# q of the first half batch by a hardware queue and cast on ScalarE, q of the last batch by crossbar, key pieces of batch 3 spread, last rows split: a fused Sinkhorn-attention and feed-forward kernel

## Chip, cores, metric

One core of one Trainium2 chip. The metric is device time in microseconds; medians of several executions are given. Ratios are the mean time of one kernel's fast runs over the mean of the other's of the same rounds, so they are not quite the ratio of the medians beside them.

## The reference, cut

```python
# q, k, v: (4, 8, 768, 64); sort_net: (4, 8, 8, 8); 8 blocks of 96 rows
P = sort_net
for _ in range(5):
    P = P - max(P, -1);  P = exp(P)
    P = P / (sum(P, -1) + 1e-9);  P = P / (sum(P, -2) + 1e-9)
k_sorted, v_sorted = P @ blocks of k, P @ blocks of v
attn = softmax(q_b @ k_sorted_b.T / 8) @ v_sorted_b         # within each block
x = heads joined: (3072, 512)
h = relu(x @ w_in)                                          # w_in (512, 2048)
out = (s * h * h + b) @ w_out                               # w_out (2048, 512)
```

## The kernel before, the parts that matter

Tokens come in eight groups of 384 (`t`), two for each batch. `ffn1(t)` and `ffn2(t)` are the two feed-forward layers; attention pieces of later groups are hung between their matmuls by a `Queue`. To evacuate a result is to copy it out of PSUM, where matmuls leave it; a load lands when the profile has its completion count full; its readers start right behind that (q of the changed kernel at 15.84, its first cast at 15.86). Only the opening has no feed-forward work to hide behind.

```python
    sn = sk.tile([BH, NB, NB], FP)
    nc.sync.dma_start(out=sn, in_=sort_net.rearrange("b h i j -> (b h) i j"))
    kb = const.tile([128, BLK, D], BF)
    vb = const.tile([128, 128, D], BF)
    def load_q(b, part=slice(0, 128)):            # q, k, v: GpSimd's (software) queue, cast to bf16 on the way
        if b not in qr:
            qr[b] = qrp.tile([128, H, TQ, D], BF, tag="qr", name=f"qr{b}")
        nc.gpsimd.dma_start(
            out=qr[b][part].rearrange("p h t d -> p h (t d)"),
            in_=q[b].rearrange("h (p t) d -> p h (t d)", t=TQ)[part])
    # ...
    load_q(0, slice(0, 64))
    load_k(*brows(0))
    load_v(*brows(0))
    load_q(0, slice(64, 128))
    # ... masks on GpSimd (ident, emat, bmask, hmask), then the loads of the weights
    between = [lambda: zero_pad(BLK), lambda: zero_pad(BLK + 16), lambda: None,
               lambda: None, lambda: None]
    for it in range(5):                            # Sinkhorn
        nc.scalar.activation(out=sn, in_=sn, func=AF.Exp)
        between[it]()                              # other ScalarE work, in order behind the exp
        # ... seven small VectorE instructions: row sums, column sums, divisions
    # ...
    warm_up(38)                                    # matmuls of zeros, ahead of the real work
    q_half(0, "s")                                 # 48 PE transposes of q, evacuated on ScalarE
    warm_up(12)
    build_pd1()                                    # Sinkhorn result -> operand pd of the key and value matmuls
    k_piece(0, 0, 16, 1, "v")()                    # keys: 16 matmuls, evacuated on VectorE ("v") or ScalarE ("s")
    k_piece(0, 32, 16, 1, "s")()
    # ... two more key pieces, value pieces, scores, q_half(1), ... then ffn1(0)
    # the attention pieces that are hung into ffn2(2) and ffn2(3):
    at4, at5 = attn(4), attn(5)
    for i, n in enumerate((1, 4, 6)):
        at4[n] = K(3, 32 * i, 16, "vsv"[i])
    at5[1] = lambda: q_piece(3, 0, "s")
    at5[4] = lambda: q_piece(3, 2, "v")
    qu = Queue(at4 + at5, 24)
```

The softmax here doesn't subtract the row's maximum and nothing guards it: scores larger than these inputs give would overflow.

Of the kernel before, what the change touches and what calls it, by code (L numbers as in the profile page):

```python
# [9 lines left out]
FP = mybir.dt.float32  # L10
BF = mybir.dt.bfloat16
AF = mybir.ActivationFunctionType
ALU = mybir.AluOpType
# [5 lines left out]
def kernel(  # L19
# [12 lines left out]
    nc = tc.nc  # L32

    B, H, S, D = q.shape
    NB = sort_net.shape[-1]
    BLK = S // NB
    BH = B * H
    NHP = H // 2
    d_model = H * D
    d_ff = moe_w_in.shape[1]  # L40
    NF = d_ff // 128
    HB = NB // 2
    TG = HB * BLK
    NT = B * 2
    VW = D + 2
    TQ = S // 128
# [8 lines left out]
    qrp = ctx.enter_context(tc.tile_pool(name="qrp", bufs=2))  # L55
    qtp = ctx.enter_context(tc.tile_pool(name="qtp", bufs=2))
# [4 lines left out]
    gtp = ctx.enter_context(tc.tile_pool(name="gtp", bufs=2))  # L61
    osb = ctx.enter_context(tc.tile_pool(name="osb", bufs=3))
# [4 lines left out]
    psb = ctx.enter_context(tc.tile_pool(name="psb", bufs=2, space=bass.MemoryType.PSUM))  # L67
# [3 lines left out]
    sn = sk.tile([BH, NB, NB], FP)  # L71
    nc.sync.dma_start(out=sn, in_=sort_net.rearrange("b h i j -> (b h) i j"))

    kb = const.tile([128, BLK, D], BF)
    vb = const.tile([128, 128, D], BF)
    qr = {}

    def load_q(b, part=slice(0, 128)):
        if b not in qr:
            qr[b] = qrp.tile([128, H, TQ, D], BF, tag="qr", name=f"qr{b}")  # L80
        nc.gpsimd.dma_start(
            out=qr[b][part].rearrange("p h t d -> p h (t d)"),
            in_=q[b].rearrange("h (p t) d -> p h (t d)", t=TQ)[part])

    def load_k(rows, prow, n=1):
        for c0 in range(0, BLK, BLK // n):
            cs = slice(c0, c0 + BLK // n)
            nc.gpsimd.dma_start(out=kb[prow, cs, :], in_=kraw[rows, cs, :])
# [4 lines left out]
    def brows(b):  # L93
        return slice(b * 64, (b + 1) * 64), slice((b % 2) * 64, (b % 2) * 64 + 64)

    s_bc = const.tile([128, 1], FP)
# [15 lines left out]
    new_vs(1)  # L112
    nc.scalar.activation(out=warm, in_=warm, func=AF.Exp)

    load_q(0, slice(0, 64))
    load_k(*brows(0))
    load_v(*brows(0))
    load_q(0, slice(64, 128))
# [24 lines left out]
    for c0 in range(0, d_ff, FCH):  # L143
        w = const.tile([128, NHP, FCH], BF, name=f"wi{c0}")
        nc.gpsimd.dma_start(
            out=w, in_=moe_w_in.rearrange("(hp p) f -> p hp f", p=128)[:, :, c0:c0 + FCH])
# [5 lines left out]
    for f0 in range(0, NF, FW):  # L152
        w = const.tile([128, FW, d_model], BF, name=f"wo{f0}")
        nc.gpsimd.dma_start(
            out=w, in_=moe_w_out.rearrange("(f p) n -> p f n", p=128)[:, f0:f0 + FW, :])
# [7 lines left out]
    def wo_at(f):  # L163
        return wos[f // FW][:, f % FW, :]
# [4 lines left out]
    def warm_up(n):  # L169
        for _ in range(n):  # L170
            wp = psb.tile([128, 256], FP, tag="b", name="wp")
            nc.tensor.matmul(out=wp, lhsT=zt[:, 0:128], rhs=zt, start=True, stop=True)  # L172

    def zero_pad(r0):
        nc.scalar.copy(out=vb[:, r0:r0 + 16, :],
                       in_=zt[:, 0:D].unsqueeze(1).broadcast_to([128, 16, D]))
# [4 lines left out]
    nc.vector.tensor_reduce(out=rstat, in_=sn, axis=AX.X, op=ALU.max)  # L181
    nc.vector.tensor_tensor(out=sn, in0=sn, in1=rstat.broadcast_to([BH, NB, NB]),
                            op=ALU.subtract)
    between = [lambda: zero_pad(BLK), lambda: zero_pad(BLK + 16), lambda: None,
               lambda: None, lambda: None]
    for it in range(5):
        nc.scalar.activation(out=sn, in_=sn, func=AF.Exp)
        between[it]()
# [6 lines left out]
        if it == 0:  # L195
            nc.vector.tensor_scalar(out=rstat, in0=rstat, scalar1=1e-9, scalar2=None,
                                    op0=ALU.add)
# [28 lines left out]
    def evac(out, in_, eng):  # L226
        if eng == "v":
            nc.vector.tensor_copy(out=out, in_=in_)  # L228
        else:
            nc.scalar.copy(out=out, in_=in_)  # L230

    QT = {}
# [18 lines left out]
    def q_piece(b, hp0, eng):  # L251

        if hp0 == 0:
            QT[b] = qtp.tile([128, NHP, S], BF, tag="qt", name=f"qt{b}")
        ps = psa.tile([128, 2, 1024], BF, tag="a", name="tq")
        for i in range(2):
            for t in range(TQ):
                for e in range(2):
                    nc.tensor.transpose(  # L259
                        out=ps[e * 64:(e + 1) * 64, i, t * 128:(t + 1) * 128],  # L260
                        in_=qr[b][:, 2 * (hp0 + i) + e, t, :], identity=ident)
        evac(QT[b][:, hp0:hp0 + 2, :].rearrange("q a (p t) -> q a p t", t=TQ),
             ps[:, :, 0:S].rearrange("q a (t p) -> q a p t", t=TQ), eng)

    def k_piece(b, c0, nc2, nb, eng):




        pr = brows(b)[1] if nb == 1 else slice(0, 128)  # L270
        rhs = (pd1[pr] if b < 2 else pd2[pr, b - 2]).rearrange("p e m i -> p (e m i)")
        if nc2 * nb > 8:
            ps = psa.tile([128, nc2, nb * 64], FP, tag="a", name="tk")
        else:
            ps = psb.tile([128, nc2, nb * 64], FP, tag="b", name="tk")
        for c in range(nc2):
            nc.tensor.matmul(out=ps[:, c, :],  # L277
                             lhsT=kb[pr, c0 + 2 * c:c0 + 2 * c + 2, :].rearrange("p c d -> p (c d)"),
                             rhs=rhs, start=True, stop=True)
        g0 = (b % 2) * 32  # L280

        def half(cp):
            if b == 0:
                cs = slice(c0 + cp, c0 + 2 * nc2, 2)
            else:
                cs = slice(cp * (BLK // 2) + c0 // 2, cp * (BLK // 2) + c0 // 2 + nc2)
            for e in range(2):
                evac(ks[e * 64:(e + 1) * 64, g0:g0 + nb * 32, cs].rearrange(
                         "p (b g) c -> p b g c", b=nb),
                     ps[cp * 64:(cp + 1) * 64].rearrange(  # L290
                         "p c (b e g) -> p e b g c", b=nb, e=2)[:, e], eng)

        half(0)
        return lambda: half(1)
# [133 lines left out]
    GT = {}  # L428
# [22 lines left out]
    bias = const.tile([128, d_model], FP)  # L451
# [3 lines left out]
    def flush():  # L455
        while waiting:
            r0, ops = waiting.pop(0)
            ot = osb.tile([128, d_model], FP, tag="ot", name="ot")
            nc.vector.scalar_tensor_tensor(out=ot, in0=ops, scalar=s_bc, in1=bias,  # L459
                                           op0=ALU.mult, op1=ALU.add)  # L460
            nc.sync.dma_start(out=out[r0:r0 + 128, :], in_=ot)

    def ffn2(t, slot=nothing):
        gt = GT.pop(t)
        for m in range(TG // 128):
            ops = psb.tile([128, d_model], FP, tag="b", name="ops")
            for f in range(NF):
                nc.tensor.matmul(out=ops, lhsT=gt[:, f, m * 128:(m + 1) * 128],  # L468
                                 rhs=wo_at(f), start=(f == 0), stop=(f == NF - 1))
                if f % 4 == 3:  # L470
                    if f == NF - 1:
                        waiting.append((t * TG + m * 128, ops))
                        if ready:
                            flush()
                    slot()
# [22 lines left out]
    def S2(t, hp):  # L498
        return lambda: (s_piece(t, hp), s_piece(t, hp + 1))

    def P2(t, hp):
        return lambda: (p_piece(t, hp), p_piece(t, hp + 1))

    def T(t):
        return lambda: x_turn(t)

    def attn(t):
        return [S2(t, 0), nothing, P2(t, 0), S2(t, 2), nothing, P2(t, 2), nothing, T(t)]
# [9 lines left out]
    def build_pd1():  # L518
        pt = block_rows(0)
        nc.vector.tensor_tensor(  # L520
            out=pd1, in0=hmask.rearrange("p (m e) i -> p e m i", e=2),
            in1=bass.AP(tensor=pt.tensor, offset=pt.offset,
                        ap=[list(pt.ap[0]), [0, 2], [0, NHP], list(pt.ap[1])]),
            op=ALU.mult)
# [9 lines left out]
                op=ALU.mult)  # L534


    warm_up(38)
    q_half(0, "s")
    warm_up(12)
    build_pd1()  # L540
    k_piece(0, 0, 16, 1, "v")()
    k_piece(0, 32, 16, 1, "s")()
    k_piece(0, 64, 8, 1, "v")()
# [40 lines left out]
    def csums(f0, f1):  # L584
        for f in range(f0, f1):
            if f == 1:
                nc.gpsimd.tensor_tensor(out=csum, in0=wo_at(0), in1=wo_at(1), op=ALU.add)
            elif f > 1:
# [9 lines left out]
    qu = Queue([lambda: q_piece(1, 0, "s"), lambda: q_piece(1, 2, "v")]  # L598
               + [lambda c0=c0: k_piece(1, c0, 16, 1, "vsv"[c0 // 32])() for c0 in range(0, BLK, 32)]
               + [seq(lambda: load_k(*brows(2)), lambda: load_k(*brows(3)), lambda: load_q(2), bias_piece), S2(2, 0), V2[0], S2(2, 2), V2[1], V2[2], V2[3],  # L600
                  P2(2, 0), V2[4], P2(2, 2), V2[5], S2(3, 0),
                  T(2), P2(3, 0), S2(3, 2), lambda: q_piece(2, 0, "v"), P2(3, 2), T(3),
                  lambda: q_piece(2, 2, "v")], 24)
# [3 lines left out]
    def K(b, c0, nc2, eng):  # L607
        return lambda: k_piece(b, c0, nc2, 1, eng)()

    qu = Queue([nothing if i % 2 else K(2, i * 8, 8, "vs"[i // 2 % 2]) for i in range(12)]  # L610
               + [nothing] * 4, 16)
# [4 lines left out]
    v_read(2, nc.gpsimd)  # L616
    v_read(3, nc.gpsimd)
    load_q(3)
    at4, at5 = attn(4), attn(5)
    for i, n in enumerate((1, 4, 6)):  # L620
        at4[n] = K(3, 32 * i, 16, "vsv"[i])
    at5[1] = lambda: q_piece(3, 0, "s")
    at5[4] = lambda: q_piece(3, 2, "v")
    qu = Queue(at4 + at5, 24)
    ffn2(2, qu)
    ffn2(3, qu)
    ffn1(4)
# [1 line left out]
    qu = Queue(attn(6) + attn(7), 24)  # L629
# [36 lines left out]
```

## Time and profile before

| | before |
|---|---|
| median | 241.99 us |
| span of the profiled execution | 241.1 us |
| PE busy | 227.1 us (94%) |
| key matmuls of batch 0 start | 13.49 |
| first feed-forward matmul | 30.66 |
| PE clock at half speed | 14.40 to 34.88 |

Times inside a kernel are microseconds from the start of the profiled execution. PE is TensorE, DVE VectorE, ACT ScalarE, POOL GpSimd, SP the sync engine. The views that carry the argument are shown in the prediction; two lines more, from the table of windows of the kernel before (window, length, then busy time of PE, PEld, DVE, ACT, POOL, then clock, DMA share, GB/s), show the stall that the second half of the change is for: 1.23 us of PE idle in the first, 0.32 in the second.

```profile
119.00:134.00 15.00, 13.77 (x154) 7.44 (x155) 8.90 (x18) 6.24 (x9) 0.00 (x0) 1.00 0.16 46
134.00:149.00 15.00, 14.68 (x166) 8.02 (x167) 10.06 (x16) 4.45 (x5) 0.00 (x0) 1.00 0.31 80
```

### The profile page before, as it was taken

To read this page: it belongs to the slowest core of one execution; us is meant where nothing else is said; L and a number is where in the kernel's file an instruction comes from. 1 tells how busy PE (TensorE), PEld (TensorE's weight loads), DVE (VectorE), ACT (ScalarE), POOL (GpSimd) and SP (SyncE) were. 2 spreads that over 40 slices of the span, in tenths; PEclk is the share of its full clock that TensorE was granted. 3 is DMA by queue.
4 is the path that set the end of the run, shared out by engine and by line. 5 is a ranking of instruction groups with operands and counts; after the bars stand their busy time and mean duration, and the time that the engine had idled before them with its cause. 6 is when DMAs were issued, how large, how long until landed. Compare 5 with 4: busy or idle time off the path is not lost.

```text
span 241.1 us, 4882 instructions
## 1 busy us (share of the span) xinstructions
PE 227.1 (94%) x2059; PEld 136.1 (56%) x2080; DVE 134.1 (56%) x268; ACT 107.9 (45%) x154; POOL 39.2 (16%) x52
## 2 busy tenths in 40 slices
PE   8869799989999999999998999999999999999993
PEld 4468698845545555555554455666554556654441
DVE  5775547967993558766465748343353544342221
ACT  6356456435438451677626250656522225660000
POOL 7820000099960000460000000000000000000000
PEclk9965569999999999999999999999999999999998
DMA  4999999985999993599902061400014232001212
GB/s 63 187 199 212 216 201 206 219 206 103 141 153 178 273 307 97 123 120 112 146 7 87 3 152 46 109 0 3 1 52 122 67 111 45 0 3 43 82 48 87
DMA packets 29622, 27.33 MB, mean 113 GB/s; under 512 B 16928, under 2 KB 23840, under 8 KB 29088
## 3 DMA queue, kind: packets, MB, share of 16 engines
q0 software_dynamic: 8400, 15.21, 38.0%
q1 hardware_dynamic: 21200, 11.81, 20.6%
q8 instruction: 16, 0.26, 0.5%
q14 instruction: 6, 0.05, 0.1%
HBM read 29.63 MB, written 8.65 MB: 159 GB/s over the span
## 4 chain that ended last, share of the span: by engine, by line
PE 84%; DVE 6%; DMA 6%; issue 2%; POOL 1%; ACT 1%; POOLq 0%
PE hps L442 34%; PE ops L468 34%; DMA vb<-in_v_dram 6%; PE sc L358 3%; PE pv L385 3%; PE tv L303 2%; PE tk L277 2%; PE tq L259 2%; DVE x L390 2%; PE tv L333 1%; DVE gt L447 1%; DVE vn L228 1%; DVE ot L459 1%; PE tq L244 1%; DVE ks L228 1%
## 5 line engine op out<-in xcount | busy, mean ns | idle before, releaser
L442 PE MATMUL hps<-xt,wi 128*128 128x384 bf16 (+1 forms) x576 | 89.8, 313 | 1.0 <-DVE xt L228 1.0
L468 PE MATMUL ops<-wo,gt 128*128 128x512 bf16 x363 | 87.7, 380 | 1.5 <-issue 0.5
L446 ACT ACTIVATE rt<-hps 128x768 bf16<-128x768 f32 (+1 forms) x72 | 53.2, 739 | 53.7 <-PE hps L442 52.6
L442 PEld LDWEIGHTS <-wi 128*128 128x128 bf16 x576 | 54.6, 100 | 31.3 <-issue 2.3
L447 DVE TENSOR_TENSOR gt<-rt 128x768 bf16<-128x768 bf16 (+1 forms) x72 | 42.0, 585 | 42.2 <-ACT rt L446 41.8
L468 PEld LDWEIGHTS <-gt 128*128 128x128 bf16 x384 | 35.0, 98 | 38.4 <-issue 0.6
L361 ACT ACTIVATE at<-sc 96x768 bf16<-96x768 f32 x32 | 24.3, 802 | 35.2 <-PE sc L358 35.2
L459 DVE SCALAR_TENSOR_TENSOR ot<-ops,s_bc,bias 128x512 f32<-128x512 f32 x24 | 18.0, 749 | 38.0 <-PE ops L468 37.9
L390 DVE TENSOR_TENSOR x<-pv,rec 96x512 bf16<-96x512 f32 (+1 forms) x36 | 22.6, 628 | 1.3
L228 DVE CAST ks<-tk 64x512 bf16<-64x512 f32 (+1 forms) x36 | 20.9, 579 | 4.2 <-PE tk L277 3.8
L589 POOL TENSOR_TENSOR csum<-csum,wo 128x512 f32<-128x512 f32 x14 | 17.6, 1254 | 1.0
L230 ACT CAST ks<-tk 64x256 bf16<-64x256 f32 (+1 forms) x28 | 13.7, 490 | 8.0 <-PE tk L277 7.7
L385 PEld LDWEIGHTS <-at 96*128 96x128 bf16 (+1 forms) x256 | 12.3, 105 | 4.0 <-ACT qt L230 1.0
L385 PE MATMUL pv<-vs,at 96*128 96x66 bf16 (+1 forms) x256 | 13.0, 200 | 0.8 <-DVE rec L389 0.6
L358 PEld LDWEIGHTS <-ks 64*96 64x96 bf16 x256 | 8.4, 132 | 6.8 <-issue 5.0
L389 DVE RECIPROCAL rec<-pv 96x8 f32<-96x8 f32 (+1 forms) x36 | 6.9, 192 | 9.2 <-PE pv L385 9.2
L358 PE MATMUL sc<-qt,ks 64*96 64x96 bf16 x256 | 10.8, 223 | 1.0 <-DVE x L390 1.0
L172 PE MATMUL wp<-zt 128*128 128x256 bf16 x50 | 9.1, 300 | 1.1 <-DVE warm L104 1.1
L277 PEld LDWEIGHTS <-kb 64*128 64x128 bf16 x192 | 6.7, 98 | 5.4 <-issue 5.3
L277 PE MATMUL tk<-pd,kb 64*128 64x64 bf16 x192 | 8.2, 195 | 0.9 <-DVE pd L520 0.9
L230 ACT CAST vn<-tv 128x1024 bf16<-128x1024 f32 x6 | 6.1, 1012 | 4.1 <-PE tv L333 2.3
L303 PE MATMUL tv<-pd,vb 64*128 64x64 bf16 x64 | 6.0, 272 | 1.7 <-DMA vb<-in_v_dram 1.1
(67 smaller groups left out, 101.1 us busy)
## 6 DMA issues: line engine op xcount, KB each, us to landing
out_dram<-ot SPq DMA_DIRECT2D x24, 256.0 KB, 2.2
kb<-in_k_dram POOLq DMA_DIRECT2D x4, 768.0 KB, 10.1
vb<-in_v_dram POOLq DMA_DIRECT2D x4, 768.0 KB, 18.9
qr<-in_q_dram POOLq DMA_DIRECT2D x3, 768.0 KB, 19.3
wi<-in_moe_w_in_dram POOLq DMA_DIRECT2D x2, 1024.0 KB, 18.9
wo<-in_moe_w_out_dram POOLq DMA_DIRECT2D x2, 1024.0 KB, 30.1
dv<-vn SPq DMA_DIRECT2D x6, 256.0 KB, 6.6
vs<-dv POOLq DMA_DIRECT2D x4, 384.0 KB, 11.1
```

Of the source, the lines that this page charges most:

```text
L228: nc.vector.tensor_copy(out=out, in_=in_)
L230: nc.scalar.copy(out=out, in_=in_)
L277: nc.tensor.matmul(out=ps[:, c, :], lhsT=kb[pr, c0 + 2 * c:c0 + 2 * c + 2, :].rearrange("p c d -> p (c d)"), rhs=rhs, start=True, stop=True)
L358: nc.tensor.matmul(out=sc[:, e, n * BLK:(n + 1) * BLK], lhsT=ks[pr, g0 + n, :], rhs=QT[b][pr, hp, q0:q0 + BLK], start=True, stop=True)
L361: nc.scalar.activation(out=at, in_=sc[:, :, 0:TG], func=AF.Exp, scale=scale)
L385: nc.tensor.matmul(out=pv[e][0:m, (n - n0) * VW:(n - n0 + 1) * VW], lhsT=atf[:, c0:c0 + m], rhs=VS[b][:, gi, :], start=True, stop=True)
L390: nc.vector.tensor_tensor(out=x[:, n0:n0 + nn, hp * 128:(hp + 1) * 128].rearrange("p n (e d) -> p e n d", e=2), in0=pvv[:, :, :, 0:D], in1 ...
L442: nc.tensor.matmul(out=hps[:, f, 0:nt], lhsT=wi_at(hp, f0 + f), rhs=xt_at(t, hp, n0, nn), start=(hp == 0), stop=(hp == NHP - 1))
L446: nc.scalar.activation(out=rt[:, :, 0:nt], in_=hps[:, :, 0:nt], func=AF.Relu)
L447: nc.vector.tensor_tensor(out=gt[:, f0:f0 + 2, c0:c0 + nt], in0=rt[:, :, 0:nt], in1=rt[:, :, 0:nt], op=ALU.mult)
L459: nc.vector.scalar_tensor_tensor(out=ot, in0=ops, scalar=s_bc, in1=bias, op0=ALU.mult, op1=ALU.add)
L468: nc.tensor.matmul(out=ops, lhsT=gt[:, f, m * 128:(m + 1) * 128], rhs=wo_at(f), start=(f == 0), stop=(f == NF - 1))
```

## The change

The intent: free the software queue of the first half of q, so that k and v land earlier, and keep PE busy until the keys start; take PE transposes away (crossbar, the transpose in the DMA); take a stall away (spread); shorten the end (split). In the last list, `S2` and `P2` are pieces of scores and of their product with v, `K` key pieces, `T` transposes of x, and `nothing` a free slot.

```diff
+    qf = gtp.tile([64, H, TQ, D], FP, tag="gt", name="qf")
+    nc.sync.dma_start(out=qf.rearrange("p h t d -> p h (t d)"),
+                      in_=q[0].rearrange("h (p t) d -> p h (t d)", t=TQ)[0:64])
     def load_q(b, part=slice(0, 128)):
+        if b == B - 1:
+            qr[b] = qrp.tile([128, TQ, H, D], BF, tag="qr", name=f"qr{b}")
+            for t in range(TQ):
+                nc.gpsimd.dma_start(
+                    out=qr[b][:, t],
+                    in_=q[b][:, t * 128:(t + 1) * 128, :].rearrange("h p d -> p h d"))
+            return
# ...
-    load_q(0, slice(0, 64))
     load_k(*brows(0))
     load_v(*brows(0))
# ...
+    def q_cast(h0, h1):
+        nc.scalar.copy(out=qr[0][0:64, h0:h1], in_=qf[:, h0:h1])
-    between = [lambda: zero_pad(BLK), lambda: zero_pad(BLK + 16), lambda: None,
-               lambda: None, lambda: None]
+    between = [lambda: zero_pad(BLK), lambda: zero_pad(BLK + 16), lambda: q_cast(0, 3),
+               lambda: q_cast(3, 6), lambda: q_cast(6, 8)]
# ...
+    def q_turn(b):
+        QT[b] = qtp.tile([128, NHP, S], BF, tag="qt", name=f"qt{b}")
+        for t in range(TQ):
+            nc.sync.dma_start(out=QT[b][:, :, t * 128:(t + 1) * 128],
+                              in_=qr[b][:, t].rearrange("p h d -> p (h d)"), transpose=True)
# ... last_rows: the last 128 rows in columns 0:384 (stored by SP) and 384:512 (stored by ACT)
-    warm_up(38)
-    q_half(0, "s")
-    warm_up(12)
-    build_pd1()
+    warm_up(78)
+    build_pd1()
+    q_half(0, "s")
# ...
-    at4, at5 = attn(4), attn(5)   # ... (see above)
+    qu = Queue([S2(4, 0), K(3, 0, 16, "s"), nothing, P2(4, 0), nothing, S2(4, 2), nothing,
+                K(3, 32, 16, "s"), P2(4, 2), nothing, T(4), K(3, 64, 16, "v"), S2(5, 0), nothing,
+                nothing, P2(5, 0), nothing, S2(5, 2), nothing, P2(5, 2), nothing, T(5),
+                lambda: q_turn(3), nothing], 24)
```

More of the change, by code (lines that the diff above doesn't have):

```diff
@@ L72 @@
     nc.sync.dma_start(out=sn, in_=sort_net.rearrange("b h i j -> (b h) i j"))
+    qf = gtp.tile([64, H, TQ, D], FP, tag="gt", name="qf")
+    nc.sync.dma_start(out=qf.rearrange("p h t d -> p h (t d)"),
+                      in_=q[0].rearrange("h (p t) d -> p h (t d)", t=TQ)[0:64])
+    qr = {0: qrp.tile([128, H, TQ, D], BF, tag="qr", name="qr0")}
     kb = const.tile([128, BLK, D], BF)
     vb = const.tile([128, 128, D], BF)
-    qr = {}
     def load_q(b, part=slice(0, 128)):
+        if b == B - 1:
[5 more added lines that the diff above has]
+            return
         if b not in qr:
@@ L461, in flush, with last_rows @@
             nc.sync.dma_start(out=out[r0:r0 + 128, :], in_=ot)
+    def last_rows(t, m):
+        gt = GT[t]
+        r0 = t * TG + m * 128
+        for c0, c1, eng in ((0, 384, nc.sync), (384, d_model, nc.scalar)):
+            ops = psb.tile([128, d_model], FP, tag="b", name="ops")
+            for f in range(NF):
+                nc.tensor.matmul(out=ops[:, 0:c1 - c0], lhsT=gt[:, f, m * 128:(m + 1) * 128],
+                                 rhs=wo_at(f)[:, c0:c1], start=(f == 0), stop=(f == NF - 1))
+            ot = osb.tile([128, d_model], FP, tag="ot", name="ot")
+            nc.vector.scalar_tensor_tensor(out=ot[:, 0:c1 - c0], in0=ops[:, 0:c1 - c0], scalar=s_bc,
+                                           in1=bias[:, c0:c1], op0=ALU.mult, op1=ALU.add)
+            eng.dma_start(out=out[r0:r0 + 128, c0:c1], in_=ot[:, 0:c1 - c0])
     def ffn2(t, slot=nothing):
-        gt = GT.pop(t)
+        gt = GT[t]
         for m in range(TG // 128):
+            if t == NT - 1 and m == TG // 128 - 1:
+                last_rows(t, m)
+                return
             ops = psb.tile([128, d_model], FP, tag="b", name="ops")
@@ L618 @@
     load_q(3)
-    at4, at5 = attn(4), attn(5)
-    for i, n in enumerate((1, 4, 6)):
-        at4[n] = K(3, 32 * i, 16, "vsv"[i])
-    at5[1] = lambda: q_piece(3, 0, "s")
-    at5[4] = lambda: q_piece(3, 2, "v")
-    qu = Queue(at4 + at5, 24)
+    qu = Queue([S2(4, 0), K(3, 0, 16, "s"), nothing, P2(4, 0), nothing, S2(4, 2), nothing,
+                K(3, 32, 16, "s"), P2(4, 2), nothing, T(4), K(3, 64, 16, "v"), S2(5, 0), nothing,
+                nothing, P2(5, 0), nothing, S2(5, 2), nothing, P2(5, 2), nothing, T(5),
+                lambda: q_turn(3), nothing], 24)
     ffn2(2, qu)
```

## The prediction

> **What bounds the kernel now.** I read the page first (busy shares, slices), then the chain of waits in order of time, then the timeline and a table of two-microsecond windows of the opening, and last the records of DMA packets and of the granted clock that the trace holds.
>
> ```profile
> PE 227.1 (94%) x2059; PEld 136.1 (56%) x2080; DVE 134.1 (56%) x268; ACT 107.9 (45%) x154; POOL 39.2 (16%) x52
> ...
> PEclk9965569999999999999999999999999999999998
> ...
> PE 84%; DVE 6%; DMA 6%; issue 2%; POOL 1%; ACT 1%; POOLq 0%
> ```
>
> TensorE is the bound: 227.1 of 241.1 us, and 84% of the chain. So whatever takes PE instructions away after the opening is worth its own length, and work on DVE, ACT or DMA is worth nothing unless PE waits for it. The clock row shows the one stretch in which PE itself is slow: slices 3 to 6 (12 to 36 us) at about half speed.
>
> ```profile
> 2.68 13.80 DMA vb<-in_v_dram
> ...
> 123.21 0.66 issue
> 123.87 0.69 DVE ks L228
> 124.57 0.69 DVE ks L228
> 125.31 0.69 issue
> 126.00 0.75 DVE ot L459
> 126.75 0.12 DVE rec L389
> 126.90 0.70 DVE x L390
> 127.64 0.38 PE sc L358 x8
> ...
> 138.38 0.79 PE tq L259 x24
> ...
> 144.72 0.79 PE tq L259 x24
> ...
> 237.22 0.75 DVE ot L459
> ```
>
> This is the chain (start, length, what). Four places of it are what the change aims at: the first v of batch 0 that lands at 16.48; a stretch from 123.2 to 127.6 where PE hangs on VectorE, which evacuates a key piece of batch 3 ahead of the softmax division; two groups of 24 PE transposes of q of batch 3; and the last eviction at 237.22.
>
> ```profile
> 8.15 0.83 PEld L244 LDWEIGHTS <-qr 64*64 64x64 bf16 x48 [0.32 <-DMA qr<-in_q_dram]
> 13.49 1.99 PE L277 MATMUL tk<-pd,kb 64*128 64x64 bf16 x48 [0.90 <-DVE pd L520]
> 14.15 4.91 DVE L228 CAST ks<-tk 64x512 bf16<-64x512 f32 x8 [0.71 <-PE tk L277]
> 16.62 4.38 PE L303 MATMUL tv<-pd,vb 64*128 64x64 bf16 x47 [1.15 <-DMA vb<-in_v_dram]
> ```
>
> The timeline of the opening: q is there at 8.15, the Sinkhorn result (pd) lets the key matmuls start at 13.49, and v comes at 16.6. But the VectorE row tells that v is less of a bound than the chain says: DVE evacuates keys until 19.06 and could not have taken a v piece before. The opening's pace is set by the key start (call it T = 13.49) and by evacuations; the first feed-forward matmul comes at 30.66, T + 17.2.
>
> ```profile
> 12.00:14.00 2.00, 0.91 (x20) 0.89 (x21) 0.71 (x4) 0.00 (x0) 0.88 (x1) 1.00 0.99 211
> 14.00:16.00 2.00, 1.47 (x36) 1.31 (x32) 1.82 (x3) 1.33 (x2) 0.00 (x0) 0.60 1.03 167
> 34.00:36.00 2.00, 2.00 (x25) 1.92 (x24) 1.25 (x5) 0.69 (x3) 0.00 (x0) 0.78 1.25 208
> ```
>
> In the windows (after the colon pair: length, busy PE, PEld, DVE, ACT, POOL, then clock, DMA share, GB/s) PE is under half busy from 12 to 14, and the clock falls right after. The clock records put it at full from 4.16 to 14.40 and at half from 14.40 to 34.88.
>
> [...] from 47 to 50 us the packet records have 54 hardware packets of 1 KB to 48 software packets of 12 KB, nearly one for one. [...] the trace has 1.03 us for the 1024-element copy[...]. [...] here six transposes of x already land in a median of 3.9 us.
>
> **Part by part.**
>
> *q of batch 3 by crossbar.* Removes 48 PE transposes: 2 x 0.79 = 1.58 us of the chain, and their evacuations (ACT 1.44, DVE 1.76, both off the path). Adds six gathers of 128-byte pieces instead of one load (in the quiet time after 105 us) and six crossbar transposes of 128 KB, together twice the bytes of one x transpose: some 6 us estimated from 3.9. They are issued near 149 and read at 172, so hidden. Gain 1.6.
>
> *Key pieces spread.* In 119 to 134 PE is busy 13.77 of 15 us, so 1.23 idle; the next 15 us have 0.32 idle, as the ordinary rate. With two pieces on ScalarE (idle half of that time: 6.24 busy of 15) and a free slot around each, the stall should go: gain 0.9 to 1.2, say 1.0.
>
> *Last rows split.* The PE columns are the same (16 x 384 + 16 x 128 against 16 x 512). The last eviction shrinks from 512 to 128 columns. The x evictions give the slope: 0.42 us at 256 and 0.69 at 512 columns, 1.05 ns a column, so 0.75 - 384 x 1.05 ns = 0.35. Gain 0.4.
>
> Sum of these three: 3.0 us, rather sure.
>
> *The opening.* The change takes 384 KB of q out of the software queue, so k and v start first there. Their 8 packets an engine take 0.93 to 1.07 us each; k should land near 8 (was 12.2) and v near 12 (was 16.5). Then q: 512 packets of 1.5 KB, 32 an engine. They start at about 2.4 (first-packet delay of 1.0 to 1.3 us of the small sync loads), run alone for about 1 us, some 12 to 20 an engine at 60 to 80 ns, and then share one for one with k and v. So the rest either ends in the k/v stretch or just after it: landing between 9 and 14 us, where 8.2 is the value now. The casts stand on ScalarE between the exps of the Sinkhorn loop, in order: a late q holds up the fourth exp. From landing L: cast of 1152 elements 1.15 us, then two rounds of 1.75 each, so the Sinkhorn result comes at L + 4.7 (12.04 now): 14.7 for L = 10.
>
> PE now runs 78 warm-up matmuls: 14 at 0.213 (half clock) and 64 at 0.169 end at 1.13 + 3.0 + 10.8 = 15.0. That number fits a Sinkhorn end near 14.7, and I take it as a hint that L is near 10. Then T = 15.0 + 1.3 (the time from the pe matmul at 12.19 to 13.49) = 16.3, 2.8 later than now. In return v is there[...]. If it stays up, I estimate the run from T to the first feed-forward matmul as 15.0 instead of 17.2 (v pieces and scores no longer at half clock, no wait for v), and the 4.2 us of feed-forward at half clock (30.66 to 34.88) shrink to 2.1: net +2.8 - 2.2 - 2.1 = -1.5.
>
> **Rivals.** First, **the clock falls anyway**: between T + 1.5 and T + 5 PE has only v pieces to do while DVE and ACT evacuate 4.9 us of keys, and a window like that was cold before. Then only about 1.0 of the 2.2 is won, the half-clock feed-forward stays: +2.8 - 1.0 = +1.8 us, total 240.8. For it: the before kernel fell after one such window, and matmuls with 64 rows did not lift it again between 17 and 31. Against: somebody chose 78. Second, **q late becomes the wait**: L near 13 moves the Sinkhorn end to 17.7, PE idles after its warm-ups, the clock falls and T is 19: about +4.5, total 243.5. For it: the one-for-one sharing; against: the head start. Third, **PE stays warm and the evacuations are the bound**, the -1.5 case, total 237.5. A fourth, that the crossbar or the split moves a wait to SP, I hold small: SP has nothing to issue from 151 to about 173.
>
> **The range and the chances.** Opening: 0.5 x (-1.5) + 0.35 x 1.8 + 0.15 x 4.5 = +0.5. Total 241.98 - 3.0 + 0.5 = 239.5. The low end, 236.8, is the warm case with the upper sizes of the other parts; the high end, 243.5, is the late q. Faster by over 2% means under 237.1: 0.2. Slower by over 2% means over 246.8, which needs a late q and a lost part: 0.04.
>
> **What would show it.** Right: no tq group of batch 3 on PE; no PE idle around 123 to 128; a last eviction near 0.35 us; about 3 us less from 119 us to the end. For the opening: v landing near 12, the casts at 10 to 14, the key matmuls at about 16.3, and the clock at full past 14.40. Wrong: casts that wait beyond 12 us and a key start past 17 (q late); a clock row still at half from 18 to 35 (clock rival); or a first feed-forward matmul well before 30, which would mean that I have overrated the delay of T.

Where cuts are marked, sentences are out that told how the hardware behaves without a trace or run for it; what the clock would do was the author's estimate, and "it" in "If it stays up" is the clock. 241.98, less 3.0 for the three later parts, plus 0.5 for the opening (0.5 x -1.5, 0.35 x 1.8, 0.15 x 4.5), comes to 239.5 us. The 60 to 80 ns for a q packet are an estimate too: in the trace of the kernel before, the hardware queue's packets of 1 KB took 46 ns and those of 2 KB 87 (medians of its packet records). The 1.15 us for the cast of 1152 elements was measured afterwards (1.15, first cast of the changed kernel).

## More of the kernel before

The kernel before was run again beside every group of experiments; its median moved between 241.99 and 242.54 us. The groups (e1 to e4, e5 to e8, e9 and e10) ran on three different chips, so runs of different groups are compared by their ratios.

## The result, and the profile after

| | before | after | |
|---|---|---|---|
| median | 241.99 | 247.61 us | ratio 1.0237, 95% interval 1.0219 to 1.0254 |
| span of the profiled execution | 241.1 | 245.8 | +4.7 |
| key matmuls of batch 0 start | 13.49 | 22.55 | +9.06 |
| first feed-forward matmul | 30.66 | 40.15 | +9.49 |
| clock back at full speed | 34.88 | 41.88 | |
| first matmul of `ffn2(0)` | 61.33 | 69.71 | +8.38 |
| first matmul of `ffn2(2)` | 119.38 | 127.76 | +8.38 |
| first matmul of `ffn1(4)` | 149.61 | 155.03 | +5.42 |
| end of the last eviction | 237.97 | 243.02 | +5.05 |

The change is slower by 2.4%, outside the range of 236.8 to 243.5. The table, made from the chains and timelines of both traces, says where: 9.5 us are lost before the first feed-forward matmul, 1.1 come back as less of the feed-forward runs at half clock (4.2 us of it before, 1.7 after; in the kernel before, eight of its matmuls take 1.46 us at half clock and 0.83 at full), nothing changes from 61 to 119, 3.0 us are won in the stretch with batch 3, and 0.4 at the end. The first feed-forward matmuls, from the timelines of the kernel before and of the changed one (these start 0.06 us ahead of the chains' times in the table; for e1 to e10 the timelines' are given):

```profile
30.59 1.46 PE L442 MATMUL hps<-xt,wi 128*128 128x192 bf16 x8
```

```profile
40.09 1.46 PE L465 MATMUL hps<-xt,wi 128*128 128x192 bf16 x8
```

(The medians differ by 5.6 and the spans by 4.7: the profiled execution of the kernel before was 0.84 us slower than its own median.)

The page of the changed kernel: busy shares, granted clock in 40 slices, the chain by engine.

```profile
PE 230.1 (94%) x2057; PEld 138.8 (56%) x2076; DVE 129.7 (53%) x264; ACT 111.7 (45%) x160; POOL 43.0 (17%) x56
...
PEclk9995555999999999999999999999999999999999
...
PE 82%; DVE 6%; DMA 6%; ACT 2%; issue 1%; SPq 0%
```

The third slice (12 to 18 us) is now at full speed, as estimated, but four slices at half speed follow. The DMA share of the chain is as large as before, and it is another DMA. The chain in order of time shows which:

```profile
1.28 14.56 DMA qf<-in_q_dram
15.86 1.15 ACT qr L198
...
20.54 0.66 PE pe L229 x2
21.20 1.42 PE tq L260 x48
22.62 1.83 PE tk L300 x32
```

It now starts with the load of q on the hardware queue, issued at 1.28 and landing at 15.84. Its first cast on ScalarE follows at 15.86, then the rest of Sinkhorn, then the keys. The timeline of the changed kernel gives the waits (in brackets: idle time before, and what ended it):

```profile
15.86 1.15 ACT L198 CAST qr<-qf 64x1152 bf16<-64x1152 f32 x1 [8.75 <-DMA qf<-in_q_dram]
...
16.92 0.25 ACT L203 ACTIVATE sn<-sn 32x64 f32<-32x64 f32 x1
...
20.54 0.66 PE L229 MATMUL pe<-sn,emat 32*128 32x64 f32 x2 [5.85 <-DVE sn L217]
...
22.55 2.74 PE L300 MATMUL tk<-pd,kb 64*128 64x64 bf16 x48
...
25.10 1.61 PE L326 MATMUL tv<-pd,vb 64*128 64x64 bf16 x16
```

ScalarE sat 8.75 us in front of the cast, and the exp behind it (L203) started only at 16.92. PE, its warm-ups done at 14.70, idled 5.85 us; the clock records have it fall to half at 17.98, so that the keys then took 2.74 us for the same 48 matmuls (1.99 before). PE no longer waits for v (it landed at 13.1, k at 8.7; 12 and 8 were predicted), and yet from the key start to the first feed-forward matmul it takes 17.6 us, where it was 17.2.

The later parts look as they were meant to. In the changed kernel's windows, shifted by the 8.4 us of delay, the stall is gone:

```profile
127.50:142.50 15.00, 14.84 (x161) 7.94 (x163) 6.75 (x16) 8.46 (x13) 0.00 (x0) 1.00 0.67 67
```

and the last eviction (chain of the changed kernel) is a short one:

```profile
242.67 0.35 DVE ot L496
```

### The profile page after: what moved, and what is told of

It is laid out like the page before. It is cut to its first block, busy times and chain, and to the rows that moved or that the text cites. A ratio compares the mean times of both kernels' runs of the same rounds, so it can differ in the third digit from the quotient of the medians.

```text
span 245.8 us, 4901 instructions
## 1 busy us (share of the span) xinstructions
PE 230.1 (94%) x2057; PEld 138.8 (56%) x2076; DVE 129.7 (53%) x264; ACT 111.7 (45%) x160; POOL 43.0 (17%) x56
## 4 chain that ended last, share of the span: by engine, by line
PE 82%; DVE 6%; DMA 6%; ACT 2%; issue 1%; SPq 0%
PE hps L465 33%; PE ops L508 32%; DMA qf<-in_q_dram 6%; PE sc L381 3%; PE pv L408 3%; PE tk L300 3%; PE tv L326 2%; PE ops L493 1%; DVE x L413 1%; PE tq L275 1%; ACT ks L246 1%; PE tq L260 1%; PE tv L356 1%; DVE gt L470 1%; DVE ks L244 1%
## 5 line engine op out<-in xcount | busy, mean ns | idle before, releaser
L465 PE MATMUL hps<-xt,wi 128*128 128x384 bf16 (+1 forms) x576 | 88.7, 310 | 1.0 <-DVE xt L244 1.0
L508 PE MATMUL ops<-wo,gt 128*128 128x512 bf16 x349 | 84.0, 379 | 1.4 <-issue 0.5
L465 PEld LDWEIGHTS <-wi 128*128 128x128 bf16 x576 | 53.8, 99 | 31.1 <-issue 2.3
L508 PEld LDWEIGHTS <-gt 128*128 128x128 bf16 x368 | 33.6, 98 | 36.8 <-issue 0.6
L482 DVE SCALAR_TENSOR_TENSOR ot<-ops,s_bc,bias 128x512 f32<-128x512 f32 x23 | 17.2, 749 | 40.4 <-PE ops L508 40.3
L244 DVE CAST ks<-tk 64x512 bf16<-64x512 f32 (+1 forms) x32 | 18.1, 566 | 2.2 <-PE tk L300 1.7
L246 ACT CAST ks<-tk 64x512 bf16<-64x512 f32 (+1 forms) x32 | 16.0, 501 | 5.3 <-PE tk L300 5.0
L628 POOL TENSOR_TENSOR csum<-csum,wo 128x512 f32<-128x512 f32 x14 | 17.6, 1254 | 1.0
L184 PE MATMUL wp<-zt 128*128 128x256 bf16 x78 | 13.6, 289 | 1.1 <-DVE warm L117 1.1
L184 PEld LDWEIGHTS <-zt 128*128 128x128 bf16 x78 | 7.6, 98 | 6.8 <-DVE warm L117 1.1
L300 PE MATMUL tk<-pd,kb 64*128 64x64 bf16 x192 | 9.0, 203 | 0.0
## 6 DMA issues: line engine op xcount, KB each, us to landing
vb<-in_v_dram POOLq DMA_DIRECT2D x4, 768.0 KB, 15.8
```

The lines of the kernel that those rows point to most:

```text
L184: nc.tensor.matmul(out=wp, lhsT=zt[:, 0:128], rhs=zt, start=True, stop=True)
L244: nc.vector.tensor_copy(out=out, in_=in_)
L246: nc.scalar.copy(out=out, in_=in_)
L300: nc.tensor.matmul(out=ps[:, c, :], lhsT=kb[pr, c0 + 2 * c:c0 + 2 * c + 2, :].rearrange("p c d -> p (c d)"), rhs=rhs, start=True, stop=True)
L465: nc.tensor.matmul(out=hps[:, f, 0:nt], lhsT=wi_at(hp, f0 + f), rhs=xt_at(t, hp, n0, nn), start=(hp == 0), stop=(hp == NHP - 1))
L508: nc.tensor.matmul(out=ops, lhsT=gt[:, f, m * 128:(m + 1) * 128], rhs=wo_at(f), start=(f == 0), stop=(f == NF - 1))
```

## The experiments

The theory after the two traces: everything lost is lost in the opening, because the hardware queue's q lands at 15.8; it lands late because its 512 packets of 1.5 KB take turns, one for one, with the 12 KB packets of k and v on the software queue, which got there first; and it does harm because its casts stand in ScalarE's order ahead of the exps. The DMA packet records of the changed kernel agree (packets started in each stretch):

```
us        software queue       q on the hardware queue (1536 B)
2 to 4    17 of 12288 B          1
4 to 7    47 of 12288 B         45
8 to 11   46 of 12288 B         48
12 to 15  347 of 768 B         318
```

The first q packet starts at 3.98, the first k packet at 2.68. Rivals: a hardware-queue load of this form is slow by itself; q's landing bounds the opening through its transposes, wherever the casts stand; the later parts win nothing and the clock made the difference.

### e1: the old opening, the three other parts kept

```diff
-    qf = ...; nc.sync.dma_start(out=qf ...)      # and the casts in `between`
+    load_q(0, slice(0, 64))                      # ahead of load_k, as before
-    warm_up(78); build_pd1(); q_half(0, "s")
+    warm_up(38); q_half(0, "s"); warm_up(12); build_pd1()
```

> The changed kernel with its opening put back (q of the first half batch by the software queue, 50 warm-ups, no casts on ScalarE); crossbar, spread key pieces and split last rows kept. My theory after the two traces: the whole loss is in the opening (first feed-forward matmul 30.66 before, 40.15 after), and the three other parts win about 3.4 us (2 tq groups 1.6, stall 1.2, last eviction 0.4, plus some). So 238.3 to 238.9 us. Rival: the other parts win nothing and the difference comes from the shifted clock; then 241.5 to 242.

Measured: 238.22 us, ratio 0.9833 (0.9809 to 0.9858). The median is just under the expected range. The three later parts win 1.7%; the loss is in the opening. This is the fastest kernel by its median.

### e2: the new opening alone

The kernel before with `qf`, the casts and the 78 warm-ups, nothing else of the change.

> The kernel before with the opening of the change alone. My theory: 247.6 + 3.4 = 251 us, first feed-forward matmul at 40.1, q landing at 15.8. Rival (parts interact): something else than the sum of 247.6 and the gain of the run with the old opening.

Measured: 252.53 us, ratio 1.0416 (1.0391 to 1.0441), first feed-forward matmul at 40.35, first cast at 16.12. It is a little more than expected. The parts add up: -1.67% and +4.16% give +2.5%, and the change as a whole measured +2.4%.

### e3: the casts behind the Sinkhorn loop

```diff
-    between = [..., lambda: q_cast(0, 3), lambda: q_cast(3, 6), lambda: q_cast(6, 8)]
+    between = [..., lambda: None, lambda: None, lambda: None]
     # after the loop:
+    q_cast(0, 4); q_cast(4, 8)
-    q_half(0, "s")            # moved from before the key pieces ...
     k_piece(0, 80, 8, 1, "s")()
+    q_half(0, "s")            # ... to behind them
```

> The changed kernel with the three q casts moved out of the Sinkhorn loop to right behind it on ScalarE, and the q transposes behind the key pieces. q still lands at 15.8. Theory (the late q acts by standing in ScalarE's order ahead of the exps): Sinkhorn ends near 12.2, the pe matmul starts when the 78 warm-ups end at 14.7, key matmuls at 16.0 instead of 22.55, the first feed-forward matmul 4.5 to 6.5 earlier (ScalarE still has 3.1 us of casts ahead of its keys), the time 241.5 to 243.5. Rival (q's landing itself bounds the opening through its transposes, wherever the casts stand): first feed-forward matmul within 2 us of 40.15, time 246 or more.

Measured: 244.29 us, ratio 1.0077 (1.0057 to 1.0098). Key matmuls at 16.13 as expected, first feed-forward matmul at 36.41, 3.7 earlier than in the changed kernel; 4.5 to 6.5 were expected, so the time is 0.8 above its range. The timeline of this run:

```profile
16.27 2.85 ACT L198 CAST qr<-qf 64x1536 bf16<-64x1536 f32 x2 [5.65 <-DMA qf<-in_q_dram]
...
19.16 0.85 PE L263 MATMUL tq<-ident,qr 64*64 64x64 bf16 x24 [0.81 <-ACT qr L198]
```

Both explanations hold in part: of the 9.06 us by which the keys came late, 6.4 go with the order on ScalarE; but 2.7 of the 6.4 come back as new waits. ScalarE has 2.85 us of casts just when it should evacuate keys, and PE waits for a cast (0.81), for ScalarE's keys (0.57) and for its evacuation of the q transposes (1.74). As two things were moved, the casts and the transposes, the share of each in the 2.7 is not shown.

### e4: a head start for q

GpSimd's masks (`ident`, `emat`, `bmask`, `hmask`) are written ahead of `load_k(*brows(0))`, so the software queue's first load is issued at 4.10 instead of 1.31. Nothing else moves.

> The changed kernel with GpSimd's masks (3.3 us) ahead of its first loads, so that q on the hardware queue runs alone at first. Theory (q is late because its 1.5 KB packets take turns one for one with 12 KB packets of k and v that got there first): q lands at 6 to 7 instead of 15.84, the casts wait for nothing, Sinkhorn ends near 12.2, key matmuls at 16.0 (bound by the 78 warm-ups), k lands near 10.5 and v near 15; time 240 to 241.5. Rival (a hardware-queue load of this form is slow by itself): q lands at 10 or later, even without rivals on the engines, and the time stays over 243.

Measured: 241.86 us, ratio 0.9978 (0.9957 to 1.0000). The timeline of this run:

```profile
8.21 1.15 ACT L198 CAST qr<-qf 64x1152 bf16<-64x1152 f32 x1 [1.24 <-DMA qf<-in_q_dram]
...
14.68 0.40 PE L229 MATMUL pe<-sn,emat 32*128 32x64 f32 x2
...
15.99 1.56 PE L300 MATMUL tk<-pd,kb 64*128 64x64 bf16 x48
```

q lands at 8.2 instead of 15.8, so the queue form is not slow by itself at that scale. The time is level with the kernel before, but not the opening: the first feed-forward matmul comes at 32.95, so moving the masks wins back 7.1 of the 9.5 us in the profiled execution (240.54 us, 1.3 below the median), and the three later parts cover the other 2.4. q is later than the 6 to 7 expected: its 512 packets took from 2.80 to 7.23, though they had the engines nearly to themselves (k's first packet started at 6.46, when 478 of q's had). The key start is now bound by the 78 warm-ups.

### e8 and e9: k in small packets, then k and v

In e8 the key tile is padded, so that each row of k lands in eight runs:

```diff
-    kb = const.tile([128, BLK, D], BF)
+    kb = const.tile([128, 8, 12 * D + 16], BF)
-            nc.gpsimd.dma_start(out=kb[prow, cs, :], in_=kraw[rows, cs, :])
+        nc.gpsimd.dma_start(out=kb[prow, :, 0:12 * D],
+                            in_=kraw[rows].rearrange("r (a c) d -> r a (c d)", a=8))
```

> The changed kernel with the key tile padded so that k lands in runs of 1536 bytes instead of 12288; nothing else moved. If packets take turns one for one, q's 32 packets an engine now pass 32 packets of k at about 0.12 us: q lands at 10.5 to 11.5 instead of 15.84, Sinkhorn ends near 15.5, key matmuls near 17, time 241.5 to 242.5. If instead the engines share by bytes, or the hardware queue is just slow when the software queue is busy, q lands at 14 or later and the time stays over 245.

Measured: 248.69 us, ratio 1.0256 (1.0230 to 1.0282); the first cast at 15.80. By the landing this was a miss. The packet records split it: q's packets did go as the theory had it (494 of 512 had started by 11.0, where it was 125 in the changed kernel; the last ended at 11.94), but q landed only at 15.78, 3.8 us later, when the software queue had gone over to the 12 KB packets of v. That made a new theory, that the completion takes turns too, and e9 to test it: v of batch 0 in four loads with runs of 3072 bytes.

```diff
-    load_v(*brows(0))
+    load_v(*brows(0), 4)      # four loads of 24 rows of each block
```

> As the run with small k packets, and v of batch 0 in four loads with runs of 3072 bytes (about 0.24 us a packet instead of 0.95). There q's data had ended at 11.9 but its completion count was full only at 15.78. If the completion also takes turns behind software packets, it now comes within some four turns of 0.25 us: q lands at 12 to 13.5, key matmuls at 18 to 19.5, time 243.5 to 245. If the completion is slow for another reason, q lands at 15 or later again and the time stays over 247.

Measured: 245.96 us, ratio 1.0132 (1.0096 to 1.0168). The first casts of e8 and of e9, from their timelines:

```profile
15.80 1.15 ACT L197 CAST qr<-qf 64x1152 bf16<-64x1152 f32 x1 [8.55 <-DMA qf<-in_q_dram]
```

```profile
13.35 1.15 ACT L198 CAST qr<-qf 64x1152 bf16<-64x1152 f32 x1 [6.32 <-DMA qf<-in_q_dram]
```

The data ended at nearly the same time (11.94 and 12.18), the casts could start 2.5 us apart: from the last data to the landing it took 1.2 us beside packets of 3 KB, 3.8 beside 12 KB, and in the changed kernel itself, beside 768 bytes, 0.6. (In e4, where k's 12 KB packets had only just begun, it was 1.0.) So in these runs, with other packets on the other queue, q's data ended at another time (11.94 in e8, 15.25 in the changed kernel) and the landing came after another delay. The packet records have something in that stretch, too. Behind q the hardware queue has records of 4 bytes; which of them belong to which load they do not tell. In e8, 18 of them took 0.9 to 1.0 us and 14 took 1.8 to 1.9; in e9, 17 took 0.26 to 0.31 and 13 took 0.49 to 0.56; in e4 and in the changed kernel all 304 took under 0.1. A packet of v took 0.97 us in e8 and 0.25 in e9, so each of these records took as long as one or two packets of the other queue. The key start, 20.05, is later than expected (18 to 19.5), and the time is 1 us over: the clock had fallen by 17.03 and the pe matmul and key start ran at half speed. Whether q's landing waits for such records, and why some take as long as two packets, the runs do not settle; that the completion takes turns is not shown beyond the delays above.

### e10: the head start with 64 warm-ups

```diff
-    warm_up(78)
+    warm_up(64)
```

> As the head-start run, with 64 warm-ups instead of 78 (they end near 12.6, when Sinkhorn ends at 12.75). Theory (there the key start at 15.99 waited for the warm-ups and for nothing else): key matmuls at 14.1, first feed-forward matmul at 31.1 instead of 32.95, about 1.5 to 1.9 us less than that run, ratio to before 0.989 to 0.992; that is still no better than the run with the old opening (0.9833), as v's earlier landing is worth nothing. Rival (the warm-ups pay for themselves by the clock): no gain or a loss against that run, ratio 0.997 or more. Second rival (v's earlier landing is worth something once the key start is not late): ratio 0.983 or less.

Measured: 239.21 us, ratio 0.9856 (0.9829 to 0.9883). Timeline of this run, key start and first feed-forward matmul:

```profile
14.21 1.56 PE L300 MATMUL tk<-pd,kb 64*128 64x64 bf16 x48
...
31.20 1.46 PE L465 MATMUL hps<-xt,wi 128*128 128x192 bf16 x8
```

Both come where they were expected, 1.8 us earlier than in e4. The ratio is better than the range given, though it shares an interval with e1 (0.9833), so the two are not told apart by time, and the second rival (0.983 or less) is not excluded by time alone. By the traces the mended opening is 0.8 us behind the old one (31.20 against 30.44 in e1). From key start to first feed-forward matmul it takes 17.0 us here with v landing 1.5 us after the key start, and 16.9 in e1 with v landing 2.8 after it: v's earlier landing shows no gain. The two are no clean pair, though: here ScalarE has 1.5 us of q evacuations just behind the key start, which in e1 stand before it, and PE waits 1.38 us for ScalarE's keys. What speaks against a gain is VectorE: it goes from its keys to its first piece of v without a wait in both, 5.7 us after the key start here and 5.6 in e1.

### e5, e6, e7: the three other parts alone

Each is the kernel before with one part: the crossbar (`load_q` of batch 3, `q_turn` behind `T(5)`, the two `q_piece` calls out); the spread list, with the two `q_piece` calls in free slots; `last_rows`.

> The kernel before with q of batch 3 by the crossbar alone. Theory (PE is the bound there, so its own length is won): 2 x 0.79 = 1.6 us less, and 0.2 to 0.4 more where the transposes' buffers or weight loads held PE up: ratio 0.992 to 0.994. Rival (the run with the old opening got its 4 us from the stall and the split, the crossbar's work is paid back by a later wait): ratio 0.998 or more.

> The kernel before with the key pieces of batch 3 spread (two on ScalarE, a slot for each) and the q transposes kept in free slots. Theory: the stall of 123.2 to 127.6 goes, 1.0 to 1.3 us: ratio 0.9945 to 0.996, and PE idle in 119 to 134 falls from 1.23 to about 0.3. Rival (the spread needs the slots that the q transposes leave, alone it only moves the stall): ratio 0.998 or more.

> The kernel before with the last 128 rows split into 384 and 128 columns alone. Theory: the last eviction falls from 0.75 to 0.35 us and the last store is a quarter as large: 0.4 to 0.7 us, ratio 0.997 to 0.9985. Rival ([...]PE pays for 16 more weight loads): ratio 1.000.

| | median | ratio to before | |
|---|---|---|---|
| e5 crossbar | 240.98 us | 0.9937 (0.9913 to 0.9960) | -1.5 us |
| e6 spread | 241.00 us | 0.9951 (0.9930 to 0.9971) | -1.2 us |
| e7 split | 241.98 us | 0.9981 (0.9960 to 1.0002) | -0.5 us, not clear of noise |

The last column is (ratio - 1) x 242.4. The first two came out as their theories had it; e7's median ratio lies in its range, but its interval holds its rival's 1.000 as well. Multiplied, the three give 0.987, against 0.9833 for e1. The window of the spread run shows the idle time gone (0.11 of 15 us, 1.23 before):

```profile
119.00:134.00 15.00, 14.89 (x175) 8.12 (x176) 7.44 (x16) 7.65 (x13) 0.00 (x0) 1.00 0.27 66
```

A part of the scatter is the clock: with the same opening, its return to full speed lay at 34.88 (before), 35.13 (e7), 33.79 (e5), 32.84 (e1) and 32.53 (e6) in the profiled executions. Up to 2.6 us of feed-forward at half or full clock, 1.3 us of time, hang on that phase, so the 0.9 us between e1 and the sum of the parts is no interaction shown.

## Why the prediction was wrong, step by step

- **The three later parts** were predicted at 3.0 us (1.6, 1.0, 0.4). Alone they measured 1.5, 1.2 and 0.5 (the last not clear of noise), together 4.0 (e1). Right, a little low.
- **The step that failed** is "They start at about 2.4 ..., run alone for about 1 us, some 12 to 20 an engine". There was no head start: the first packet of k started at 2.68, the first of q at 3.98, when 17 of k's 64 had started, and not one q packet had run alone. From there the one-for-one sharing that the prediction had read off the trace did the rest: 32 packets an engine, against 8 of k and v and 24 more of the next load. The estimate of 9 to 14 for the landing became 15.84. In e4, with a head start of 3.7 us, q landed at 8.2. But the rate was too high as well: there, with the engines free, 77 packets started in the first 1 us, 5 an engine, and a q packet took 0.12 us on average, not 60 to 80 ns. At that rate (an estimate) even 1 us alone would have left most of q to the sharing. e8 bears out the sharing itself: with k in packets as small as q's, q's data ended at 11.94 instead of 15.25; the further 3.8 us to its landing at 15.78 there were not in the prediction at all. Nor did the hardware queue start faster in these runs: its first q packet came 1.5 us after the start of its issue with the engines free (1.27 to 2.80, e4), the software queue's first k packet 1.4 us after (1.31 to 2.68, changed kernel).
- **The hint** "That number fits a Sinkhorn end near 14.7, and I take it as a hint that L is near 10" was no evidence. The number 78 was not fitted to what the chip does: e4 and e10 show that even with q in time 14 of the 78 were too many, by 1.8 us.
- **The formula behind it held**: Sinkhorn's end was put at L + 4.7 (L is the landing of q); 15.84 + 4.7 is 20.5, and the pe matmul started at 20.54. So the mechanism of the second rival was right ("q late becomes the wait"), and its size wrong: key start 22.55 instead of 19, as L was 3 us later than its 13 and the last steps ran at half clock. A chance of 0.15 was too little for what the packet records had said.
- **v's wait**: the prediction said that DVE, not v, set the pace, and then still credited 2.2 us to the run from key start to feed-forward in the warm case. By the timelines that run is 17.5 in the changed kernel, 17.0 in e4 and e10, 16.9 in e1 and 17.1 before: no gain shows, with the reserve said at e10.
- **The clock**: the rival that it falls anyway was right in every run, also with q in time (17.98 in e4, 18.08 in e10). The 2.1 us for feed-forward at full clock were won in full by no kernel (half-clock feed-forward lasts 4.2 us before, 2.4 in e1, 1.7 in the changed kernel). The reading behind it, that the clock had fallen because PE had too little work (0.91 of 2.00 us from 12 to 14 in the kernel before), does not stand as the cause either: in e4 PE was at its 78 warm-ups from 1.13 to 14.72 and then, almost without a break, at matmuls of 64 rows and fewer, and the clock still fell at 17.98:

```profile
14.68 0.40 PE L229 MATMUL pe<-sn,emat 32*128 32x64 f32 x2
...
15.01 0.94 PE L260 MATMUL tq<-ident,qr 64*64 64x64 bf16 x48
...
15.99 1.56 PE L300 MATMUL tk<-pd,kb 64*128 64x64 bf16 x48
...
17.55 1.56 PE L326 MATMUL tv<-pd,vb 64*128 64x64 bf16 x16
```

Nor did it rise in the kernel before while PE worked from 16.62 to 21.00 on value matmuls of 64 rows (4.38 us, x47, at half clock): there it was back at 34.88, 4.2 us after the first feed-forward matmul. What moves the clock, these runs do not settle.

- **"SP has nothing to issue from 151 to about 173"**, so that the crossbar is hidden: right, e5's chain shows no new wait. Its six transposes landed in 2.4 to 4.2 us each, the last one issued at 158.0, and were first read past 170; some 6 us together had been estimated, and issuing alone took longer (150.4 to 158.0).

## What to carry to other kernels

Here the loads on two DMA queues took turns by packets, not by bytes (48 of 1536 bytes to 46 of 12288 from 8 to 11 us): the many small ones finished last, and in e8 their landing came 3.8 us after the last of their data. So see that what is needed first also starts first (e4), or that the other queue's packets are small (e8 and e9; e9 won back a part). Do not put an instruction that waits for a DMA on an engine ahead of a latency chain, here Sinkhorn's exps on ScalarE: it cost 6.4 us of key start (e3). Before you pay for removing a wait in the chain, see whether the engine behind it was free: v's wait stood first in the chain, and an earlier v showed no gain (e10).
